# Attention: phi multiplied on POOL ahead of the inverses' spreading, its transposition and that of the inverses exchanged

## The chip, the cores and the metric

The kernel runs on one core of one Trainium2 chip. Its engines work side by side, each on its own queue of instructions in order: TensorE (PE: matrix products and transpositions into PSUM), VectorE (DVE), ScalarE (ACT), GpSimd (POOL) and SyncE (SP, which issues most DMAs). Semaphores tell one engine that another has finished. The metric is device microseconds (us) of one execution; the time before is the median of three runs.

## The reference, cut to what matters

Three stages follow each other: an attention with a memory term, a mixture of experts with one expert for each token, and a dense mixture with normalised weights. The change lies in the first, and this is all of it that it computes:

```python
B, H, S, D = 4, 8, 576, 64
scores = scale * np.matmul(q, k.transpose(0, 1, 3, 2))
scores = np.where(causal, -1000000000.0, scores)
a = np.exp(scores - scores.max(-1, keepdims=True))
a /= a.sum(-1, keepdims=True) + 1e-09
local = np.matmul(a, v)
q_p = np.where(q > 0, q, np.exp(q) - 1.0) + 1.0          # phi
mem_ret = np.einsum('bhsd,bhde->bhse', q_p, M_prev)
mem_norm = np.einsum('bhsd,bhd->bhs', q_p, z_prev)[..., None] + 1e-06
out = g * (mem_ret / mem_norm) + (1 - g) * local         # g = sigmoid(beta), one number a head
```

## The kernel before, in words

The attention works on 16 pairs of heads (u = 0 to 15; a batch has four). The 576 rows of a pair are four tiles of 128 and a tail of 64. A loop of 17 iterations is pipelined by one pair: iteration u computes the scores of pair u, the transpositions and the output product of pair u-1, and loads and prepares q, k and phi of pair u+1. An iteration has five steps, n = 0 to 4. Each step begins with a tile of scores (`score`, row tiles 3, 2, 1, 0 and the tail): PE multiplies (L233) and adds the mask (L235), DVE takes the row maximum (L237), ACT exponentiates and sums (L239).

The softmax isn't normalised before the output product. The unnormalised probabilities are transposed (`ptrans`, parts 0 to 7; L268, L276, L283, L289), phi is multiplied beforehand by the row's sum, the two products are added up in PSUM (`av`: L298 with the transposed phi `pT`, L306 with the transposed probabilities `pt`), and DVE multiplies the result by the transposed inverse sums `R` (L307). So two small tables are needed for the pair before: `pT` from phi, and `R` from the inverses `rr`, which POOL spreads over 64 columns a head. Both are made from `phi_c`, called at the end of iteration u-1, and each takes four transpositions on PE and an eviction from PSUM on ACT: `inverse` (L173, L174) at n = 1 and `trans(u - 1, 2)` (L191, L209) at n = 2.

For the next pair, `phi_a` makes phi: exp on ACT (L126), max(q, 0) on POOL (L127), then on DVE min(exp, 1) + max (L128), then the product with z on POOL (L131), which `phi_b` sums (L149, L150). The table of phi, `qp`, has two buffers in turn: L127 for pair u+1 writes the one that held pair u-1, so it can't begin before the transpositions of phi of pair u-1 (L191) have read it.

All transpositions and the output products of the attention share four PSUM buffers. The first part of the output product takes one of them, the parts of `ptrans` and the transposed q (evicted half by ACT, L206, half by DVE, L207) take others, so PE waits at a transposition until the buffer it is given has been evicted. By the semaphores of the built program, in an ordinary iteration L283 waits for the ACT eviction of part 2 (L270), L289 for L207, and the first L298 for the DVE eviction of part 3 (L270), and for `pT` as well where PE has not yet seen it.

The order inside the loop is not written out: a scheduler at build time puts each engine's instructions in a queue, by its own estimate of when operands are there. On the chip the queues are fixed. After each batch (in iterations 4, 8 and 12) POOL also issues four or five indirect DMAs that scatter tokens (L395); they stand in its queue ahead of L127 of the next iteration.

The lines that the change touches, in words of the kernel before: L162 makes the inverses of the sums (DVE), L164 spreads them (POOL, 128x512), L165 multiplies the memory's factor by the sums (DVE), and L167 multiplies phi by it (POOL, 128x512).

Of the kernel before, what the change touches and what calls it, by code (L numbers as in the profile page):

```python
# [14 lines left out]
ALU = mybir.AluOpType  # L15
# [3 lines left out]
B, H, S, D = 4, 8, 576, 64  # L19
# [8 lines left out]
def attention(ctx, tc, q, k, v, M_prev, z_prev, beta, xT, ident, router=None):  # L28
    nc = tc.nc
# [55 lines left out]
    zt, ld, ph, un = {}, {}, {}, {}  # L85
# [10 lines left out]
    def load_b(b):  # L96
        zt[b] = nat.tile([128, DM], F32, tag="z", name="zb", bufs=2)
        nc.sync.dma_start(zt[b], z_prev[b].rearrange("h d -> (h d)")[None, :].to_broadcast([128, DM]))
        for h in range(2):
            src = M_prev[b].rearrange("(a two) d e -> two d a e", two=2)[h]  # L100
            nc.sync.dma_start(Mb[b % 2][h * 64:(h + 1) * 64, :, h * 64:(h + 1) * 64], src)

    def load(u, names):

        b, a = divmod(u, NP)
        for nm in names:
            src = {"k": k, "q": q, "v": v}[nm]
            t = nat.tile([128, NT, 128], F32, tag=nm, name=f"{nm}n")
            for h in range(2):
                nc.sync.dma_start(t[:, :4, h * 64:(h + 1) * 64],  # L110
                                  src[b, 2 * a + h, :512, :].rearrange("(i p) d -> p i d", p=128))
            nc.sync.dma_start(t[:64, 4].rearrange("p (h d) -> p h d", h=2),
                              src[b, 2 * a:2 * a + 2, 512:, :].rearrange("h p d -> p h d"))
            ld[u, nm] = t
# [42 lines left out]
    def phi_c(u):  # L157

        su, n = un[u]["su"], nrm[u % 2]
        nc.vector.tensor_scalar(su[:, :4], su[:, :4], 1e-9, None, ALU.add)  # L160
        rc = sm.tile([128, 4, 2], F32, tag="rc", name="rc", bufs=2)
        nc.vector.reciprocal(rc, su[:, :4])  # L162
        rr = un[u]["rr"] = tmp.tile([128, 4, 128], F32, tag="rr", name="rr")
        nc.gpsimd.tensor_copy(rr.rearrange("p i (h d) -> p i h d", h=2), rc[:, :, :, None].to_broadcast([128, 4, 2, D]))  # L164
        nc.vector.tensor_tensor(n[:, :4], n[:, :4], su[:, :4], ALU.mult)  # L165
        pv = ph[u][1][:, :4].rearrange("p i (h d) -> p i h d", h=2)
        nc.gpsimd.tensor_tensor(pv, pv, n[:, :4, :, None].to_broadcast([128, 4, 2, D]), ALU.mult)  # L167

    def inverse(u):

        p = ps_t.tile([128, 512], F32, tag="t", name="rp_")
        for i in range(4):
            nc.tensor.transpose(p[:, i * 128:(i + 1) * 128], un[u]["rr"][:, i], ident)  # L173
        nc.scalar.copy(Rs[u % 2][:, :512], p)  # L174

    def phi_t(u):
        if "pT" not in un[u]:
            un[u]["pT"] = tr.tile([128, S], F32, tag="pT", name="pT")
        return un[u]["pT"]

    def trans(u, part):


        qt = qTp[u % 2]
        p = ps_t.tile([128, 512], F32, tag="t", name="tp")
        if part == 0:
            un[u] = {"kT": tr.tile([128, S], F32, tag="kT", name="kT"), "P": {}}
        if part < 3:
            src = (ld.get((u, "k")), ld.get((u, "q")), ph[u][1] if u in ph else None)[part]
            for i in range(4):  # L190
                nc.tensor.transpose(p[:, i * 128:(i + 1) * 128], src[:, i], ident)  # L191
        else:
            src = []
            if part == 3:
                src += [ld[u, "k"], ld[u, "q"]]
                if u > 0:
                    src.append(ph[u - 1][1])
            else:
                src += [ph[u][1]]
            for n, t in enumerate(src):  # L200
                nc.tensor.transpose(p[:, n * 64:(n + 1) * 64], t[:64, 4], ident[:64, :64])

        if part == 0:
            nc.vector.tensor_copy(un[u]["kT"][:, :512], p)
        elif part == 1:
            nc.scalar.activation(qt[:, 256:512], p[:, 256:], AF.Copy, scale=0.125)  # L206
            nc.vector.tensor_scalar(qt[:, :256], p[:, :256], 0.125, None, ALU.mult)  # L207
        elif part == 2:
            nc.scalar.copy(phi_t(u)[:, :512], p)  # L209
        elif part == 3:  # L210
            nc.vector.tensor_copy(un[u]["kT"][:, 512:], p[:, 0:64])
            nc.scalar.activation(qt[0:64, 512:576], p[0:64, 64:128], AF.Copy, scale=0.125)
            nc.vector.tensor_scalar(qt[64:128, 576:640], p[64:128, 64:128], 0.125, None, ALU.mult)
            if u > 0:
                nc.vector.tensor_copy(phi_t(u - 1)[:, 512:], p[:, 128:192])
        else:
            nc.vector.tensor_copy(phi_t(u)[:, 512:], p[:, 0:64])

    def score(u, i):

        b, a = divmod(u, NP)
        kT = un[u]["kT"]
        qt = qTp[u % 2]
        s = ps_s.tile([128, 2, 512], F32, tag="s", name="s")
        nm = sm.tile([128, 2], F32, tag="nm", name="nm")
        if i == 3:
            un[u]["su"] = sm.tile([128, NT, 2], F32, tag="su", name="su", bufs=2)
        sums = un[u]["su"][:, i]
        if i < 4:
            w = (i + 1) * 128  # L230
            for h in range(2):
                r = slice(h * 64, (h + 1) * 64)
                nc.tensor.matmul(s[:, h, :w], qt[r, i * 128:(i + 1) * 128], kT[r, :w], start=True, stop=False)  # L233
            for h in range(2):
                nc.tensor.matmul(s[:, h, w - 128:w], idb, mk, start=False, stop=True)  # L235
            P = pp.tile([128, 2, w], F32, tag=f"P{i}", name=f"P{i}")
            nc.vector.tensor_reduce(nm, s[:, :, :w], AX.X, ALU.max, negate=True)  # L237
            for h in range(2):
                nc.scalar.activation(P[:, h], s[:, h, :w], AF.Exp, bias=nm[:, h:h + 1], accum_out=sums[:, h:h + 1])  # L239
        else:  # L240
            w = 288
            for h in range(2):
                nc.tensor.matmul(s[:, h, :w], qt[:, 512:640], kT[:, h * w:(h + 1) * w], start=True, stop=(h == 0))
            nc.tensor.matmul(s[:, 1, 224:288], idb, mk2, start=False, stop=True)
            P = pp.tile([128, 2, w], F32, tag=f"P{i}", name=f"P{i}")
            nc.vector.tensor_reduce(nm[:, 0:1], s[:, :, :w], AX.XY, ALU.max, negate=True)
            nc.scalar.activation(P, s[:, :, :w], AF.Exp, bias=nm[:, 0:1], accum_out=sums[:, 0:1])
        un[u]["P"][i] = P
# [72 lines left out]
    for u in range(NU + 1):  # L321
        sc, ex = u < NU, u > 0
        if u + 1 < NU:
            load(u + 1, "v")
        if u + 2 < NU:
            if (u + 2) % NP == 0:
                load_b((u + 2) // NP)
            load(u + 2, "kq")
        if u == 2 and rt:
            rt.clear()  # L330
        for n in range(5):
            if sc:
                score(u, (3, 2, 1, 0, 4)[n])
                if n == 4:
                    phi_c(u)
            if ex:
                if n == 0:
                    norm(u - 1)
                    ptrans(u - 1, 5)
                    ptrans(u - 1, 4)  # L340
                elif n < 3:
                    ptrans(u - 1, 2 * n - 2)
                    ptrans(u - 1, 2 * n - 1)
                    if n == 1:
                        inverse(u - 1)
                    else:
                        trans(u - 1, 2)
                elif n == 3:
                    ptrans(u - 1, 6)
                    ptrans(u - 1, 7)  # L350
                    av(u - 1, 0)
                else:
                    av(u - 1, 1)
                    if rt and u % NP == 0:
                        rt.batch(u // NP - 1, ps_t)
            if sc:
                if n == 0:
                    phi_b(u)
                elif n == 2:
                    gate_v(u)  # L360
                elif n == 3 and u + 1 == NU:
                    trans(u, 4)
            if u + 1 < NU:
                if n < 2:
                    trans(u + 1, n)
                elif n == 3:
                    trans(u + 1, 3)
                    phi_a(u + 1)
        if ex:
            del un[u - 1]  # L370
# [918 lines left out]
```

## Time and profile before

| what | us |
|---|---|
| median of three runs | 2078.39 (2077.78 to 2081.22) |
| the profiled execution | 2079.47 |
| its span | 2077.8 |
| PE busy, whole span | 2041.4 (98%) |
| DVE busy | 1482.1 (71%) |
| ACT busy | 854.6 (41%) |
| POOL busy | 777.2 (37%) |

The last output product of the attention ends its last eviction at about 277 us of the span; all that follows is the two mixtures. The span is 1.67 us shorter than the execution's time, which counts what lies around it. A row of the timeline has the start in us from the span's start, the time taken, engine, line, operation, output<-input, shapes, count, and in square brackets the idle time of that engine just before, with what ended it. PEld is the loading of weights, the part of PE that a wait is seen on first.

### The profile page before, as it was taken

The numbers are of one execution on the slowest core, as the hardware profiler recorded it, in microseconds if no ns is written. First come the engines' busy times: TensorE is split into PE (matmuls) and PEld (weight loads), VectorE is DVE, ScalarE is ACT, GpSimd is POOL, SyncE is SP. The second block draws the span as 40 slices with busy tenths as digits, with TensorE's granted clock in tenths as the row PEclk, the third lists the DMA queues.
The fourth block names the chain that finished last, engine by engine and source line by source line (L and its number), as shares of the span: only waits on it lengthen the run. The fifth ranks groups of instructions, "written<-read, shape, count | busy, mean of one in ns | idle before, by whom it ended". The sixth has DMA issues, their size and how long they took to land.

```text
span 2077.8 us, 31530 instructions
## 1 busy us (share of the span) xinstructions
PE 2041.4 (98%) x11526; PEld 1770.6 (85%) x11528; DVE 1482.1 (71%) x2573; ACT 854.6 (41%) x1808; POOL 777.2 (37%) x800
## 2 busy tenths in 40 slices
PE   8999999999899999999999999999999999999998
PEld 5666569999798899889889899889988889889987
DVE  7787757666786776667786677677678676677775
ACT  5556546555634333333343333333334433333332
POOL 6666511000133344344464334334345333333432
PEclk8999999999999999999999999999999999999999
DMA  7332147665612233444432222222223222222221
GB/s 189 87 71 78 33 152 231 203 212 170 209 52 61 62 69 73 61 66 77 61 106 68 61 74 69 62 73 70 62 61 112 62 63 80 61 63 80 62 62 40
DMA packets 238520, 187.35 MB, mean 90 GB/s; under 512 B 71440, under 2 KB 194320, under 8 KB 238352
## 3 DMA queue, kind: packets, MB, share of 16 engines
q1 hardware_dynamic: 229008, 171.48, 30.2%
q0 software_dynamic: 3520, 9.46, 1.3%
q10 hardware_dynamic: 5824, 4.25, 0.7%
q8 instruction: 95, 1.56, 0.3%
q14 instruction: 73, 0.60, 0.1%
HBM read 171.51 MB, written 13.64 MB: 89 GB/s over the span
## 4 chain that ended last, share of the span: by engine, by line
PE 46%; issue 16%; POOL 8%; DVE 3%; ACT 1%; POOLq 0%; DVEq 0%; ACTq 0%
PE y L1093 24%; PE prod L1022 21%; POOL T L914 4%; POOL w1l L908 3%; DVE u L1036 0%; DVE w2l L908 0%; DVE c L1036 0%; POOL out_dram L395 0%; DVE hl L1045 0%; PE lq L1134 0%; DVE S2l L908 0%; DVE A11l L908 0%; DVE A12l L908 0%; DVE csum L1167 0%; ACT hh L1040 0%
## 5 line engine op out<-in xcount | busy, mean ns | idle before, releaser
L1040 ACT ACTIVATE hh<-c 128x384 fp32r<-128x384 f32 x384 | 202.1, 526 | 837.5 <-DVE c L1036 837.4
L908 POOL TENSOR_TENSOR w1l<-T,w1h 128x1024 fp32r<-128x1024 f32 x94 | 226.9, 2414 | 850.2 <-ACT w1h L908 850.2
L1093 PE MATMUL y<-w2h,hh 128*128 128x512 f32 x1152 | 453.4, 394 | 0.0
L1093 PE MATMUL y<-w2l,hh 128*128 128x512 f32 x1152 | 453.3, 394 | 0.0
L1093 PE MATMUL y<-w2h,hl 128*128 128x512 f32 x1152 | 452.5, 393 | 0.0
L1045 DVE SCALAR_TENSOR_TENSOR hl<-c,hh 128x384 fp32r<-128x384 f32 x384 | 415.7, 1100 | 1.4 <-ACT hh L1040 1.0
L1036 DVE TENSOR_TENSOR c<-prod,u 128x384 f32<-128x384 f32 x288 | 160.2, 556 | 157.2 <-PE prod L1022 156.6
L1093 PEld LDWEIGHTS y<-w2h,hh 128*128 128x128 f32 x1152 | 216.2, 188 | 32.8
L1093 PEld LDWEIGHTS y<-w2h,hl 128*128 128x128 f32 x1152 | 216.2, 188 | 28.6
L1093 PEld LDWEIGHTS y<-w2l,hh 128*128 128x128 f32 x1152 | 216.3, 188 | 28.0
L914 POOL TENSOR_TENSOR T<-r,T 128x256 f32<-128x256 f32 x188 | 157.9, 840 | 14.0 <-issue 6.9
L914 POOL TENSOR_TENSOR T<-r 128x256 f32<-128x256 f32 x188 | 159.1, 847 | 7.2
L1036 DVE TENSOR_TENSOR u<-prod,u 128x384 f32<-128x384 f32 x192 | 106.0, 552 | 58.1 <-PE prod L1022 57.6
L1036 DVE TENSOR_TENSOR u<-prod,p 128x384 f32<-128x384 f32 x96 | 53.5, 557 | 126.9 <-PE prod L1022 126.7
L908 DVE TENSOR_TENSOR w2l<-r,w2h 128x512 fp32r<-128x512 f32 x188 | 137.0, 729 | 0.5 <-ACT w2h L908 0.5
L908 ACT CAST w2h<-r 128x512 fp32r<-128x512 f32 x188 | 106.7, 610 | 0.0
L908 DVE TENSOR_TENSOR w1l<-r,w1h 128x512 fp32r<-128x512 f32 (+1 forms) x188 | 104.7, 557 | 0.0
L1036 DVE TENSOR_TENSOR c<-prod,p 128x384 f32<-128x384 f32 x96 | 53.4, 556 | 68.9 <-PE prod L1022 64.2
L908 ACT CAST w1h<-T 128x1024 fp32r<-128x1024 f32 x94 | 97.0, 1032 | 1.0 <-POOL T L914 1.0
L1050 ACT COPY p<-prod 128x384 f32<-128x384 f32 x96 | 46.1, 480 | 121.3 <-PE prod L1022 121.3
L1104 DVE SCALAR_TENSOR_TENSOR acc<-y,P,acc 128x512 f32<-128x512 f32 x126 | 92.4, 744 | 4.3 <-PE y L1093 4.3
L908 ACT CAST w1h<-r 128x512 fp32r<-128x512 f32 (+1 forms) x188 | 94.5, 502 | 0.0
(386 smaller groups left out, 4210.4 us busy)
## 6 DMA issues: line engine op xcount, KB each, us to landing
r<-in_moe_w_dram SPq DMA_DIRECT2D x188, 512.0 KB, 4.6
r<-in_moe_w_dram SPq DMA_DIRECT2D x188, 256.0 KB, 3.0
xr<-xs_sorted SPq DMA_DIRECT2D x22, 256.0 KB, 5.1
kn<-in_k_dram SPq DMA_DIRECT2D x32, 128.0 KB, 2.7
qn<-in_q_dram SPq DMA_DIRECT2D x32, 128.0 KB, 2.8
vn<-in_v_dram SPq DMA_DIRECT2D x32, 128.0 KB, 2.6
xs_sorted<-zrow ACTq DMA_DIRECT2D x16, 256.0 KB, 3.4
zb<-in_z_prev_dram SPq DMA_DIRECT2D x4, 256.0 KB, 3.6
```

Of the source, the lines that this page charges most:

```text
L908: return (lambda: nc.scalar.copy(hi, src)), (lambda: eng.tensor_tensor(lo, src, hi.bitcast(F32), ALU.subtract))
L914: sub = lambda i, a, b: (lambda: nc.gpsimd.tensor_tensor(T[:, i], a, b, ALU.subtract))
L1022: nc.tensor.matmul(p, a[:, kd], b[:, kd], start=(i == 0), stop=(i == 5))
L1036: nc.vector.tensor_tensor(st[o], a, st[b], ALU.add)
L1040: nc.scalar.activation(hh[:, f, a * HT:(a + 1) * HT], st[o], AF.Relu)
L1045: nc.vector.scalar_tensor_tensor(hl[:, f, w], st[o], 0.0, hh[:, f, w].bitcast(F32), ALU.max, ALU.subtract)
L1050: nc.scalar.copy(st["p1"], p)
L1093: nc.tensor.matmul(yt[t], a[:, f, t * 128:(t + 1) * 128], b[:, f], start=(j == 0 and f == 0 and i == 0), stop=(j == NJ - 1 and f == 1 and ...
L1104: nc.vector.scalar_tensor_tensor(acc[t], yt[t], P[:, m, e:e + 1], acc[t], ALU.mult, ALU.add)
```

## The change

In `phi_c` the product of phi and its factor is put ahead of the spreading of the inverses, on DVE and on POOL. In the loop the two calls are exchanged: `trans(u - 1, 2)` is made at n = 1 and `inverse(u - 1)` at n = 2. No instruction is added or taken away.

```diff
         nc.vector.tensor_scalar(su[:, :4], su[:, :4], 1e-9, None, ALU.add)
+        nc.vector.tensor_tensor(n[:, :4], n[:, :4], su[:, :4], ALU.mult)
+        pv = ph[u][1][:, :4].rearrange("p i (h d) -> p i h d", h=2)
+        nc.gpsimd.tensor_tensor(pv, pv, n[:, :4, :, None].to_broadcast([128, 4, 2, D]), ALU.mult)
         rc = sm.tile([128, 4, 2], F32, tag="rc", name="rc", bufs=2)
         nc.vector.reciprocal(rc, su[:, :4])
         rr = un[u]["rr"] = tmp.tile([128, 4, 128], F32, tag="rr", name="rr")
         nc.gpsimd.tensor_copy(rr.rearrange("p i (h d) -> p i h d", h=2), rc[:, :, :, None].to_broadcast([128, 4, 2, D]))
-        nc.vector.tensor_tensor(n[:, :4], n[:, :4], su[:, :4], ALU.mult)
-        pv = ph[u][1][:, :4].rearrange("p i (h d) -> p i h d", h=2)
-        nc.gpsimd.tensor_tensor(pv, pv, n[:, :4, :, None].to_broadcast([128, 4, 2, D]), ALU.mult)
...
                     if n == 1:
+                        trans(u - 1, 2)
+                    else:
                         inverse(u - 1)
-                    else:
-                        trans(u - 1, 2)
```

On PE, in iteration 7, the four transpositions of the inverses (`rr`, L173) and the four of phi (`qp`, L191) change places; this is the place at n = 1:

```order
 L268 MATMUL tp2_1666<-ident_58,P2_1468 128x128
 L268 MATMUL tp2_1666<-ident_58,P3_1430 128x128
-L173 MATMUL rp__1672<-ident_58,rr_1582 128x128 x4
+L191 MATMUL tp_1672<-ident_58,qp_1370 128x128 x4
 L191 MATMUL tp_1678<-ident_58,qn_1419 128x128 x4
 L233 MATMUL s_1685<-kT_1456,qTp1_136 128x256 x2
```

Nothing else moves there; the transpositions of the inverses stand at n = 2, where those of phi stood, and all other rows of PE in this iteration keep their places.

On DVE the scheduler gives a new order. In iteration 7, `qp_1750` is phi of pair 8, the next one, `tp_1678` the transposed q, `tp2_1700` part 3 of the transposed probabilities, `nm_1686` the maximum of the scores of n = 2:

```order
 L237 TENSOR_REDUCE nm_1651<-s_1650 128x2
 L270 COPY pt_1625<-tp2_1666 128x512
+L128 SCALAR_TENSOR_TENSOR qp_1750<-ex_1749,qp_1750 128x512
+L128 SCALAR_TENSOR_TENSOR qp_1750<-ex_1749,qp_1750 64x128
 L237 TENSOR_REDUCE nm_1686<-s_1685 128x2
 L207 TENSOR_SCALAR qTp0_134<-tp_1678 128x256
 L270 COPY pt_1625<-tp2_1700 128x384
-L128 SCALAR_TENSOR_TENSOR qp_1750<-ex_1749,qp_1750 128x512
+L149 TENSOR_REDUCE nrm0_142<-ex_1749 128x8
 L237 TENSOR_REDUCE nm_1714<-s_1713 128x2
 L285 COPY pt_1625<-tp2_1723 128x4x64
 L290 COPY pt4_1626<-tp2_1730 64x128
```

Both rows of L128 have moved from behind the evictions L207 and L270 to ahead of them. The same order stands in iterations 3, 4, 6, 7, 8, 10, 11, 12 and 14. In iteration 2 the two rows keep their places. In iteration 1 the long one goes ahead of L237 and L207 as here, and L149 too goes ahead of L207.

In iterations 5, 9 and 13, behind a batch's scatter, DVE's queue changes thus (iteration 5; `qp_1370` is phi of pair 6, `tp_1298` the transposed q):

```order
 L237 TENSOR_REDUCE nm_1271<-s_1270 128x2
 L270 COPY pt_1245<-tp2_1286 128x512
+L128 SCALAR_TENSOR_TENSOR qp_1370<-ex_1369,qp_1370 128x512
+L207 TENSOR_SCALAR qTp0_134<-tp_1298 128x256
 L237 TENSOR_REDUCE nm_1306<-s_1305 128x2
-L207 TENSOR_SCALAR qTp0_134<-tp_1298 128x256
 L270 COPY pt_1245<-tp2_1320 128x384
-L128 SCALAR_TENSOR_TENSOR qp_1370<-ex_1369,qp_1370 128x512
+L128 SCALAR_TENSOR_TENSOR qp_1370<-ex_1369,qp_1370 64x128
 L237 TENSOR_REDUCE nm_1334<-s_1333 128x2
```

Here the long row of L128 alone has moved ahead of L207; POOL's queue, in which L127 stands behind the scatter, is as it was. In iterations 1, 5, 9 and 13 it is L283 that waits for L207 in the changed program, and no longer L289.

## Rows read from the trace of the kernel before

**Rows 1.** Busy time by stretch: PE, PEld, DVE, ACT, POOL, PEclk, DMA share, GB/s.
```profile
120.00:160.00 40.00, 39.11 (x287) 24.35 (x284) 31.16 (x88) 22.95 (x67) 22.86 (x27) 1.00 0.29 68
```
**Rows 2.** The view of waits: who waited for whom, us in total, times, longest.
```profile
DVE qp L128 <- POOL qp L127: 19.6, 14, 2.5
...
PEld x L298 <- ACT pT L209: 8.1, 15, 1.8
```
**Rows 3.** Timeline of iteration 7, all engines, from n = 1 to n = 3.
```profile
124.68 0.47 PEld L173 LDWEIGHTS rp__1672<-ident,rr 128*128 128x128 f32 x4
124.74 0.39 POOL L142 TENSOR_TENSOR vn<-vn,om 64x128 f32<-64x128 f32 x1
...
126.72 0.69 DVE L237 TENSOR_REDUCE nm<-s 128x2 f32<-128x512 f32 x1 [1.03 <-PE s L235]
...
127.07 0.47 PEld L191 LDWEIGHTS tp<-ident,qp 128*128 128x128 f32 x4
...
127.33 0.41 DVE L207 TENSOR_SCALAR qTp<-tp 128x256 f32<-128x256 f32 x1
...
127.66 0.55 DVE L270 COPY pt<-tp 128x384 f32<-128x384 f32 x1
...
127.93 1.98 POOL L127 TENSOR_SCALAR qp<-qn 128x512 f32<-128x512 f32 x2 [2.79 <-issue]
...
128.20 0.42 PEld L283 LDWEIGHTS tp<-ident,P 128*128 128x128 f32 x4
...
128.59 0.11 PEld L289 LDWEIGHTS tp<-ident,P 128*64 128x64 f32 x1
...
128.99 0.30 PEld L298 LDWEIGHTS x<-pT,Mb 128*128 128x128 f32 x2 [0.29 <-ACT pT L209]
...
129.46 0.77 DVE L128 SCALAR_TENSOR_TENSOR qp<-ex,qp 128x512 f32<-128x512 f32 x1 [1.25 <-POOL qp L127]
...
130.30 1.27 POOL L131 TENSOR_TENSOR ex<-qp,zb 128x512 f32<-128x512 f32 x1 [0.40 <-DVE qp L128]
...
131.01 0.71 DVE L128 SCALAR_TENSOR_TENSOR qp<-ex,qp 64x128 f32<-64x128 f32 x1
```
**Rows 4.** Groups by line and shape, 40 to 260 us: busy us, mean ns.
```profile
L127 POOL TENSOR_SCALAR qp<-qn 128x512 f32<-128x512 f32 x13 | 19.4, 1495 | 27.7 <-issue 16.4 <-PE tp L191 10.2 <-PE tp L289 1.1
```
**Rows 5.** Timeline of DVE in iteration 0, where POOL does not run L131 beside L128.
```profile
11.67 0.27 DVE L128 SCALAR_TENSOR_TENSOR qp<-ex,qp 64x128 f32<-64x128 f32 x1
11.87 0.67 DVE L149 TENSOR_REDUCE nrm<-ex 128x8 f32<-128x512 f32 x1
```
**Rows 6.** Timeline of iteration 1.
```profile
29.41 0.47 PEld L173 LDWEIGHTS rp__440<-ident,rr 128*128 128x128 f32 x4
...
30.75 1.04 POOL L141 TENSOR_TENSOR vn<-vn,om 128x512 f32<-128x512 f32 x1
...
33.83 0.42 PEld L283 LDWEIGHTS tp<-ident,P 128*128 128x128 f32 x4
```
**Rows 7.** Timeline of iteration 5, behind the first scatter.
```profile
98.38 0.60 PE L283 MATMUL tp<-ident,P 128*128 128x128 f32 x4
...
99.25 2.01 POOL L127 TENSOR_SCALAR qp<-qn 128x512 f32<-128x512 f32 x2
...
102.50 0.81 PE L298 MATMUL x<-pT,Mb 128*128 128x320 f32 x2 [0.35 <-DVE pt L290]
```
**Rows 8.** Timeline of iteration 9, behind the second scatter.
```profile
164.78 0.96 POOL L395 DMA_INDIRECT xs_sorted<-xr,row  x1 [0.30 <-ACT pt L270]
...
167.47 0.69 PE L298 MATMUL x<-pT,Mb 128*128 128x256 f32 x2 [1.57 <-ACT pT L209]
```
**Rows 9.** Timeline of iteration 15, the first without phi of a next pair.
```profile
261.98 0.30 PEld L298 LDWEIGHTS x<-pT,Mb 128*128 128x128 f32 x2 [0.81 <-ACT pT L209]
```
**Rows 10.** Timeline of PE behind the routed experts' main loop.
```profile
518.33 1.00 PE L824 MATMUL h1r<-w1l,xh 128*128 128x256 f32 x4 [1.98 <-PEq L889]
```
**Rows 11.** Busy time by stretch, directly after that wait.
```profile
518.50:522.00 3.50, 3.50 (x18) 3.50 (x18) 2.42 (x5) 2.38 (x6) 0.00 (x0) 0.51 0.81 261
```

## Prediction

> **What bounds the kernel now.** I read the busy time by stretch first. In 40 us of the attention's steady part PE is busy 39.11 at the full granted clock, while DVE, ACT and POOL have 9 to 17 us of slack each [rows 1]. So only an instruction that PE would wait for, or a loss of its clock, changes the time; the work of the other engines is free until PE stands behind it. The mixtures have no edited line and are taken as they are.
>
> The view of waits then names two things that touch the change [rows 2]. PEld's first L298 waits for ACT's eviction of the transposed phi, `pT`: 8.1 us in 15 times. That is the wait which the exchange can take away. And DVE's L128 waits for POOL's L127, 19.6 us in 14 times. Before, this second wait costs PE nothing. The timeline of iteration 7 shows why: DVE stands idle for 1.25 us ahead of L128 at 129.46, but L207 and the last L270, which free PSUM buffers for PE, were issued at 127.33 and 127.66, ahead of it in the queue [rows 3]. PE's own wait in that iteration is 0.29 us, for `pT`.
>
> **The change part by part.** No instruction is added; what counts is order. Three edits go together at nothing: the product on POOL made ahead of the spreading, the tiny DVE product, and the exchange of four transpositions for four of the same size. The first two are work of engines with slack, the third leaves PE's sum unchanged. Their bounds are 0 and, were phi late at n = 1, a wait like that for `pT`, 1.8 us at the longest [rows 2]; I take 0.
>
> What the exchange sets off is an earlier L127. It is bound to the transpositions of phi, since it overwrites the buffer that they read: they start at 127.07, L127 at 127.93, 0.86 us later [rows 3]. Put at the place of L173, which starts at 124.68, they would release it at 125.54; POOL is free by then, as L142 ends at 124.74 + 0.39 = 125.13. The long L127 takes 1.49 us [rows 4], so phi's maximum is there at 127.03. That is 2.4 us earlier, but the new order puts both rows of L128 ahead of L237, L207 and L270 of DVE, where before they came behind them. L237 began at 126.72. Now it must wait for L128, and behind it wait L207 and L270, and behind these PE's L289 and L298.
>
> Ordinary iterations (3, 4, 6, 7, 8, 10, 11, 12 and 14: nine), by the durations of [rows 3]:
> - L128 long starts 127.07 (0.04 after L127, as before: 129.46 against 127.93 + 1.49), takes 0.77; a next row on DVE begins 0.08 before its predecessor ends (127.33 against 126.72 + 0.69), so L128 short begins at 127.76. It takes 0.27 when POOL doesn't work beside it [rows 5]: 128.03.
> - L237 0.69 less 0.08: 128.64. L207 0.41: to 128.97. L270 0.55 less 0.08: to 129.44; by the 0.08 not always gained, to 129.52. Before, L270 ended at 128.21.
> - PE's L289 stood at 128.59 and goes to some 129.05, and L298, which needs that L270, goes from 128.99 (its 0.29 for `pT` included) to about 129.57: +0.58. Nine times: **+5.2 us**.
> Bounds: if PE does not wait at all it gains the 0.29, -2.6 us over nine; from above, L128 short takes 0.71 beside POOL's L131 as it did at 131.01 [rows 3], +0.44 each, +9.2 us in all. I stay at 0.27, because it would now be issued just ahead of L131 and not behind it.
>
> Iteration 1: PE's first transpositions of the slot start at 29.41, but POOL is busy with L141 up to 30.75 + 1.04 = 31.79 [rows 6]. L127 ends at 33.28, its short row (1.98 - 1.49 = 0.49) at 33.77, L142 and L155 at 0.39 each at 34.55, L131 (1.27) at 35.82, L149 (0.67 [rows 5]), now ahead of L207, at 36.53, L207 at 36.86. L283, which now waits for L207, goes from 33.83 [rows 6] to 36.91: **+3.1**.
>
> Iteration 5: L127 stands behind the scatter and keeps its 99.25 [rows 7]. It ends at 100.74, L128 at 101.55, L207 at 101.88, and L283 starts at 101.93 where PE had it at 98.38: 3.6 late. Later in the iteration a wait of 0.35 for L290 [rows 7] and one of 0.3 for `pT` are absorbed: **+3.0**.
>
> Iterations 9 and 13: L395 ends at 164.78 + 0.96 = 165.74 [rows 8]; L127 to 167.27, L128 to 168.08, L207 to 168.41, L283 at 168.46 and L298 0.50 behind it (128.20 to 128.99 less 0.29 [rows 3]) at 168.96. Before, L298 started at 167.47 after waiting 1.57 for `pT`, a wait that goes [rows 8]: +1.5. Iteration 13 has the same order and I give it the same: **+3.0** for both. Bounds for these four iterations together: 0, if PE finds other buffers free, to 13, if each costs the whole 3.1 to 3.6.
>
> Gains where no L128 stands in the way: 0.81 in iteration 15 [rows 9], about 0.29 each in 2 and 16: **-1.4**. Sum so far: 5.2 + 3.1 + 3.0 + 3.0 - 1.4 = **+12.9 us**.
>
> The clock: in the steady part it is granted in full [rows 1], so it can't gain. Four waits of some 3 us are new on PE. The nearest row is the wait of 1.98 us in the experts' stage [rows 10], behind which the clock was granted at 0.51 (1.2 GHz in place of 2.4) for 3.5 us [rows 11], that is 1.7 us lost. So 0 to 4 x 1.7 = 6.8 us; I take two falls, for the two longest waits (iterations 1 and 5): **+3.4**. The total is +16.3. The sum is made on the profiled execution, 2079.47 us (span 2077.8), 0.05% above the median of 2078.39; added to the median it gives **2095 us**.
>
> A rule that speaks against this change: the short L128 is a DVE instruction with two inputs in SBUF, and POOL's L131 reads SBUF; the row of L128 that ran beside L131 took 0.71 us [rows 3] where the one without took 0.27 [rows 5]. The Trainium skill, SBUF — State Buffer, "Who interferes with whom", says that such a pair contends for a shared read port, that this is an exclusive lock, and that the order of issue decides who blocks. The trace agrees that DVE is slowed; that it can be shut out for all of L131's 1.27 us no row here shows. If DVE is first, the sum stays; if POOL is first, it is the first rival below.
>
> **The rivals.**
> 1. POOL gets ahead at L128 short. L131 would start some 0.07 us after L128 long ends, at 127.91, and last to 129.18; L128 short would end 1.2 us later than in my sum, and with it L207 and L270. Nine times 1.2 is +10.8: 2106 us. For it: the 0.71 at 131.01 [rows 3]. Against: DVE's next row starts without a gap, POOL's needs a semaphore. Chance 0.16.
> 2. Faster: the exchange does what is wanted. `pT` is a slot earlier, the 8.1 us of PEld's wait [rows 2] go, and L128 finds its input there, so that no eviction is late: 2070 us. It decides if L127 ends before 125.95 or so, when L128's 0.77 could be over by L237's 126.72. With 125.54 + 1.49 it misses that by 1.1 us, unless POOL is released sooner than 0.86 us after the slot's start or PE runs later against POOL than in this trace. Chance 0.08.
> 3. No change: L207 and L270 are late but PE has other work up to them in ordinary iterations, so the 0.29 each is gained (-2.6, and -1.4 in iterations 2, 15 and 16), and only the iterations 1, 5, 9 and 13 lose, about half of my 9.1, with no fall of the clock: +0.6, 2079 us. For it: four PSUM buffers in turn. Against: each is wanted again within a step. Chance 0.12.
>
> **How the numbers follow.** My forecast has 0.64: 2095, by itself 2087 (no fall of the clock, ordinary iterations at less than 0.2) to 2102 (four falls, some L128 at 0.71). What the measurement of this kernel can tell is about 0.2%, 4.2 us. Faster has rival 2, 0.08. Same has rival 3 and the weakest end of the forecast: 0.13. Slower has the rest, 0.79. The range goes from 2080 to 2107: it takes in rival 1 at its upper end and leaves out rival 2, most of rival 3, and a little above.
>
> **What would show it.** Right: in iteration 7 DVE's idle time ahead of L128 stands before L237, not after L270; PE waits at L289 or L298 for DVE's L207 or L270, about 0.6 us; L298's wait for `pT` is gone from the view of waits; in iterations 1 and 5 L283 waits about 3 us for L207, perhaps with half the clock behind it. The two mixtures keep their length. Wrong: L127 starting much sooner or later than 0.86 us after the slot; no PE wait on L207 or L270; L128 short at 1.2 us or more (rival 1); the waits as I say but a span within 4 us of before, which would mean that PE makes up later what it loses here.

## The result, and the profile after

The changed kernel takes 2096.75 us (median of four runs, 2094.83 to 2097.15), the kernel before beside it 2078.27 (four runs); the ratio is 1.0083, 95% interval 1.0071 to 1.0095. The forecast was 2095, slower. The profiled execution has a span of 2095.4 us, 17.6 more than before.

I take the start of DVE's first L270 in each iteration as its mark and set the marks of the two traces side by side. By the mark of iteration 16, 17.2 of the 17.6 us have arisen, 0.45 of them ahead of the mark of iteration 1; the mixtures, behind the last L307, take 1801.7 us, and took 1800.9 before. The ordinary place first: the timeline of iteration 7 after the change, all engines.

```profile
134.93 0.47 PEld L191 LDWEIGHTS tp<-ident,qp 128*128 128x128 f32 x4
...
135.77 0.40 POOL L142 TENSOR_TENSOR vn<-vn,om 64x128 f32<-64x128 f32 x1
...
136.13 1.98 POOL L127 TENSOR_SCALAR qp<-qn 128x512 f32<-128x512 f32 x2
...
137.65 0.97 DVE L128 SCALAR_TENSOR_TENSOR qp<-ex,qp 128x512 f32<-128x512 f32 x2 [1.72 <-POOL qp L127]
...
138.55 0.67 DVE L237 TENSOR_REDUCE nm<-s 128x2 f32<-128x512 f32 x1
139.15 0.40 DVE L207 TENSOR_SCALAR qTp<-tp 128x256 f32<-128x256 f32 x1
139.48 0.54 DVE L270 COPY pt<-tp 128x384 f32<-128x384 f32 x1
139.60 0.11 PEld L289 LDWEIGHTS tp<-ident,P 128*64 128x64 f32 x1 [0.74 <-DVE qTp L207]
...
140.07 0.30 PEld L298 LDWEIGHTS x<-pT,Mb 128*128 128x128 f32 x2 [0.35 <-DVE pt L270]
```

The idle time of DVE ahead of L128 has moved from behind L270 [rows 3] to ahead of L237, and grown from 1.25 to 1.72 us. Behind it everything is late in a row: L237, L207, L270, and so PE's L289 and L298. By the slot I mean the place at n = 1 where the exchanged transpositions stand. L298 starts 5.14 us after the slot's first row here, 4.31 before (128.99 against 124.68 in [rows 3]). L127 starts 1.20 us after the slot and not 0.86, because POOL's L142 ends only at 136.17. In this, iteration 7 is one of two exceptions: in seven of the nine ordinary iterations L127 starts 0.86 or 0.87 us after the slot's first row, in iteration 11 it starts 1.34 us after it.

The view of waits of the changed kernel (who waited for whom, us in total, times, longest):

```profile
DVE qp L128 <- POOL qp L127: 29.9, 14, 5.2
...
PE tp L283 <- DVE qTp L207: 13.4, 4, 3.7
...
PEld tp L289 <- DVE qTp L207: 4.4, 9, 0.9
...
PEld x L298 <- DVE pt L270: 3.2, 9, 0.4
```

The wait of L298 for `pT` [rows 2] has no row any more. In its place stand nine waits for L207 and L270, in the nine ordinary iterations, and four long ones of L283, in iterations 1, 5, 9 and 13. Iteration 5, behind the scatter:

```profile
103.28 0.96 POOL L395 DMA_INDIRECT xs_sorted<-xr,row  x1 [0.30 <-issue]
104.27 2.01 POOL L127 TENSOR_SCALAR qp<-qn 128x512 f32<-128x512 f32 x2
105.83 0.77 DVE L128 SCALAR_TENSOR_TENSOR qp<-ex,qp 128x512 f32<-128x512 f32 x1 [5.16 <-POOL qp L127]
106.53 0.41 DVE L207 TENSOR_SCALAR qTp<-tp 128x256 f32<-128x256 f32 x1
...
107.09 1.08 PE L283 MATMUL tp<-ident,P 128*128 128x128 f32 x4 [3.68 <-DVE qTp L207]
```

L283's four transpositions take 1.08 us here and 0.60 before [rows 7]: the clock has fallen. Busy time by stretch, of the stretches behind the four waits (PE, PEld, DVE, ACT, POOL, PEclk, DMA share, GB/s):

```profile
37.00:41.00 4.00, 3.48 (x16) 2.23 (x16) 2.06 (x8) 1.37 (x7) 0.45 (x1) 0.57 0.22 76
105.50:112.50 7.00, 5.41 (x21) 3.64 (x22) 5.23 (x16) 3.00 (x12) 3.10 (x5) 0.51 0.06 14
180.50:184.50 4.00, 4.00 (x17) 2.49 (x16) 2.76 (x12) 2.26 (x10) 1.50 (x2) 0.57 0.30 66
249.00:252.50 3.50, 3.33 (x15) 2.19 (x15) 2.73 (x8) 2.07 (x9) 1.49 (x2) 0.51 0.00 0
```

The clock fell to half at each of the four waits, in the wait or up to 1.5 us behind its end; before, the attention had full clock from 27.5 us on.

### The profile page after: what moved, and what is told of

The parts are those of the page before. It is cut to its first block, busy times and chain, and to the rows that moved or that the text cites. A ratio compares the mean times of both kernels' runs of the same rounds, so it can differ in the third digit from the quotient of the medians.

```text
span 2095.4 us, 31517 instructions
## 1 busy us (share of the span) xinstructions
PE 2047.7 (98%) x11526; PEld 1776.4 (85%) x11528; DVE 1468.4 (70%) x2573; ACT 855.3 (41%) x1808; POOL 779.7 (37%) x800
## 4 chain that ended last, share of the span: by engine, by line
PE 45%; issue 16%; POOL 8%; DVE 3%; ACT 0%; POOLq 0%; ACTq 0%; DVEq 0%
PE y L1093 24%; PE prod L1022 21%; POOL T L914 4%; POOL w1l L908 3%; DVE u L1036 0%; DVE w2l L908 0%; DVE c L1036 0%; POOL out_dram L395 0%; DVE hl L1045 0%; DVE S2l L908 0%; DVE A11l L908 0%; DVE A12l L908 0%; PE lq L1134 0%; DVE csum L1167 0%; PE lg L1146 0%
```

## The experiments

Eleven kernels ran, each beside the kernel before. Theory A is the prediction's: DVE stands still at L128 for POOL, the evictions stand behind it, PE waits for them, and its clock falls behind the long waits. Where a diff says `behind` or `after_all`, it adds an ordering edge without a semaphore: the scheduler must put the one DVE instruction later in the queue than the other, and nothing waits for anything new.

**Holding L128 behind the eviction, in all iterations, in four, in the rest.**

```diff
-            nc.vector.scalar_tensor_tensor(p, e, 1.0, p, ALU.min, ALU.add)
+            behind(u, nc.vector.scalar_tensor_tensor(p, e, 1.0, p, ALU.min, ALU.add))
...
+    def behind(u, i):
+        if u > 1: after_all(tc, i, late, mybir.DependencyClass.NoSync)
```

Here u is the pair whose phi is made, one ahead of the iteration, and `late` holds DVE's eviction of part 3 of the same iteration (the line that fills it is left out). The second run has `u % 4 == 2 and u > 1` as its condition, the third `u % 4 != 2 and u > 1`.

All: 

> The changed kernel, with one thing added: an ordering edge without a semaphore puts both rows of L128 behind the DVE eviction of part 3 (L270) of the same iteration, from iteration 1 on. PE's order is the same as in the changed kernel; POOL, ACT and DVE keep their instructions. Theory A (the loss comes from L128 standing ahead of the evictions L207 and L270 on DVE while its input from POOL is late, with the clock's falls behind the long waits): the whole loss goes, and the wait for pT stays away; 2072 to 2079 us, no L283 or L289 waiting for L207, full clock from 28 to 300 us. Rival B (the exchange itself costs: the inverses a slot later, so that L307 and the x buffer are late, or POOL's new order): most of the loss stays, 2090 us or more, with waits on L307 or on R.

Four: 

> The changed kernel with L128 held behind L270 only in iterations 1, 5, 9 and 13; the others keep the changed order. Theory A: the four long waits (3.0 to 3.7 us each in the trace of the changed kernel) and the four stretches at half clock go, the ordinary waits of about 0.5 us stay: 2097 less 12 to 14, 2083 to 2085 us. If the clock's falls cost nothing (rival C: PE behind the wait is bound by other engines anyway): only the waits' 10 us less what the kernel before waited there, 2088 to 2090. Rival B: 2094 or more.

The rest: 

> The complement: L128 held behind L270 in all iterations but 1, 5, 9 and 13. Theory A: the ordinary 0.5 us in nine iterations and the wait for pT go, the four long waits and their clock stay: 2097 less 5 to 8, 2089 to 2092 us. Together with the other half the two savings should add up to that of holding all, within 3 us. Rival B: 2094 or more.

| held in | us, median | ratio to before, 95% |
|---|---|---|
| all iterations | 2068.45 | 0.9951 (0.9938 to 0.9965) |
| 1, 5, 9, 13 | 2077.86 | 0.9990 (0.9981 to 0.9999) |
| the others | 2086.12 | 1.0037 (1.0023 to 1.0050) |

The kernel before had 2079.54 beside them. PE's order is the changed kernel's in all three. Holding all gives back more than the change had cost, and ends below the range expected. The exchange is kept and the loss is gone, so rival B falls. Against before the changed kernel stood at +18.5 us, the three at -11.1, -1.7 and +6.6: the four iterations are worth 20.2 us, the others 11.9, together 32.1 against 29.6, additive within the 3 us. Both parts are larger than I expected (12 to 14, and 5 to 8). By the marks, the four iterations of the second run give 18.8 us: they end 4.0 us below the kernel before, where I had brought them back no further than to it. The nine others of the third run give 8.0; the rest lies outside them, in part in iterations 5 and 13, where the profiled execution had a shorter fall of the clock and none (2.7 us together). Rival C, a clock that costs nothing, would have left the second run at 2088 to 2090. Iteration 7 with L128 held, PE and DVE:

```profile
123.32 0.41 DVE L207 TENSOR_SCALAR qTp<-tp 128x256 f32<-128x256 f32 x1
123.65 0.55 DVE L270 COPY pt<-tp 128x384 f32<-128x384 f32 x1
124.11 0.68 DVE L128 SCALAR_TENSOR_TENSOR qp<-ex,qp 128x512 f32<-128x512 f32 x1
124.58 0.11 PEld L289 LDWEIGHTS tp<-ident,P 128*64 128x64 f32 x1
...
124.69 0.30 PEld L298 LDWEIGHTS x<-pT,Mb 128*128 128x128 f32 x2
```

Neither L128 nor PE has idle time in brackets: the wait for `pT` of [rows 3] is gone and nothing has taken its place.

**Is it the place in the queue, or the late input?** L127 goes to DVE; L127 and L128 stay ahead of the evictions.

```diff
-            (nc.gpsimd if u else nc.vector).tensor_scalar(p, qn, 0.0, None, ALU.max)
+            nc.vector.tensor_scalar(p, qn, 0.0, None, ALU.max)
```

> The changed kernel with L127 moved from POOL to DVE, which has only L128's input in its own hands then; PE's order stays that of the changed kernel, and L127 and L128 still stand ahead of L237, L207 and L270 in DVE's queue in the ordinary iterations. Theory A (what costs is that DVE stands still for POOL, not that L128 takes its turn early): the idle time ahead of L128 goes, also behind the scatters, the four long waits and the clock's falls go, and what is left is DVE's own work ahead of the evictions; 2068 to 2079 us. Rival E (the mere work of phi ahead of the evictions makes them late): L127 adds to it, so 2095 or more.

Measured: 2069.61 us, ratio 0.9954 (0.9940 to 0.9967). DVE in iteration 7:

```profile
122.06 0.54 DVE L127 TENSOR_SCALAR qp<-qn 128x512 f32<-128x512 f32 x2
122.52 0.88 DVE L128 SCALAR_TENSOR_TENSOR qp<-ex,qp 128x512 f32<-128x512 f32 x2
...
123.32 0.68 DVE L237 TENSOR_REDUCE nm<-s 128x2 f32<-128x512 f32 x1
```

DVE works from 122.06 to L237 at 123.32 without a gap, on 1.3 us more than stood there before the change, and the loss is gone. So rival E falls: the early place costs nothing by itself that this run can tell, only with an input that is late. One wait and one fall of the clock were left, in iteration 9:

```profile
162.53 0.30 PEld L298 LDWEIGHTS x<-pT,Mb 128*128 128x128 f32 x2 [1.99 <-DVE pt L270]
```

```profile
164.00:168.00 4.00, 4.00 (x14) 2.29 (x14) 2.47 (x12) 1.83 (x7) 1.87 (x3) 0.57 0.35 78
```

The expectation had all falls gone. DVE stood idle for 2.20 us ahead of that L270, in the kernel before for 2.10 us at the same place, in holding all for 0.27; what it waited for is not shown.

**The two halves of the change.** Only the exchange with L128 unheld and held, and only the product first:

```diff
                     if n == 1:
-                        inverse(u - 1)
-                    else:
                         trans(u - 1, 2)
+                    else:
+                        inverse(u - 1)
```

This is the exchange alone, on the kernel before; with the hold of the first experiment it is the second run. The product alone is the other part of the change's diff, with the calls as before.

> Only the two calls are exchanged; the product of phi and its factor stays behind the spreading on POOL, as in the kernel before. PE's and ACT's orders are those of the changed kernel, and L128 stands ahead of the evictions as there. Theory A: the same loss, 2093 to 2098 us, and a wait of L191 for phi's product at n = 1 at most in the order of 1 us an iteration, since the product comes 0.6 us later. Rival D (the loss hangs on POOL's order of product and spreading): back to 2080 or less.

> Only the two calls are exchanged, with L128 held behind L270 as in the first experiment; the product of phi stays behind the spreading on POOL. Theory A: phi's product comes 0.6 us later than with the product first, and the transpositions of phi at n = 1 still find it done; within 3 us of holding all, 2067 to 2072. Rival D (the product's place on POOL carries the gain): 2076 or more, with L191 waiting for POOL at n = 1.

> Only the product of phi is put ahead of the spreading, the calls at n = 1 and n = 2 stay as before; PE's and ACT's orders are those of the kernel before. Theory A: no engine that PE waits for gains or loses, the inverses are 1 us later for transpositions that come a whole step later; 2076 to 2081, no difference that can be measured. Rival F (the inverses are now late at n = 1): 2085 or more, with L173 waiting for the spreading.

Measured: exchange alone 2099.11 (1.0089, 1.0076 to 1.0103), exchange with L128 held 2068.27 (0.9944, 0.9931 to 0.9958), product alone 2080.27 (1.0000, 0.9990 to 1.0009). The first is 1 us over the range expected. The product's place does nothing in any of them; loss and gain both hang on the exchange.

**A third buffer, and both cures at once.**

```diff
-        qp = tmp.tile([128, NT, 128], F32, tag="qp", name="qp")
+        qp = tmp.tile([128, NT, 128], F32, tag="qp", name="qp", bufs=3)
```

This stands on holding all; the second run has L127 on DVE on holding all, with two buffers.

> Holding all as in the first experiment, and a third buffer for phi, so that L127 does not wait for the transpositions of phi of the pair before. Theory A: L127 is earlier, but once L128 is behind the evictions nothing on PE waits for it; the same as holding all within 3 us, 2066 to 2071. If L127's release still cost PE time somewhere: faster by more than 4 us, 2064 or less.

> Both cures at once: L127 on DVE and L128 held behind L270. Theory A: each takes the same stall away, so they do not add up; 2066 to 2071 us, the same as either within 3 us. If the late start of L127 behind the scatters still cost something: 2064 or less.

Measured: 2068.84 (0.9944, 0.9931 to 0.9958) and 2068.53 (0.9955, 0.9942 to 0.9969). With the third buffer L127 runs an iteration earlier, and DVE's idle time ahead of L128 in iterations 5 and 9 of holding all (2.45 and 2.08 us) is gone, yet the time is the same. Once the evictions no longer stand behind L128, it does not matter when its input comes. Counting L127 on DVE and the exchange alone with L128 held, five kernels now stand at 2068 to 2070 us, about 0.5% below the kernel before and 1.3% below the changed one; none went lower.

**The clock by itself.** First a base in which the long waits of iterations 5, 9 and 13 stay (the first added line, on holding the others; `m` is the short L128, `last` the eviction L290; L149 is tied likewise, in a line left out here), then the same with idle products in them (the second added line).

```diff
+        after_all(tc, m, last if u % 4 == 2 else [], mybir.DependencyClass.NoSync); ph[u] = ex, qp
...
-                nc.tensor.matmul(s[:, h, w - 128:w], idb, mk, start=False, stop=True)
+                nc.tensor.matmul(s[:, h, w - 128:w], idb, mk, start=False, stop=True); [nc.tensor.matmul(s[:, h, 128:], zeros[:, :128], zeros[:, :384], start=True, stop=True) for _ in range(9 if i == 0 and u % 4 == 1 < u else 0)]
```

> The kernel of the third experiment (L128 held in the ordinary iterations only), with the short row of L128 and L149 also put behind L290 in iterations 1, 5, 9 and 13. There only the long row of L128 still stands ahead of L207. It is the base of the next run. Theory A: iteration 1 loses the delay by L131 and L149 (its L207 no longer waits for them), the waits of 3 us or more in 5, 9 and 13 stay, with a fall of the clock behind two or three of them; 2081 to 2085 us.

> The same, with 18 idle products of zeros (384 columns each, about 2.9 us by those of 128 columns at full clock) in PE's queue after the mask of n = 3 in iterations 5, 9 and 13, directly ahead of the L283 that waits; they write a part of the scores' buffer that nobody reads. The orders of POOL and ACT are those of the run before, DVE's differs only behind L290. If the clock's fall is a cost of its own (about 1.5 us each, as the changed order's iterations with and without a fall differ): L283 starts at the same time or up to 0.3 us later, no half clock behind it, 3 to 5 us faster than the run before. If it costs nothing, or falls all the same: within 1 us of the run before, or slower.

Measured: base 2088.15 (1.0056, 1.0041 to 1.0071), filled 2078.79 (1.0007, 0.9998 to 1.0016). The base missed its range by 3 us: all four iterations fell to half clock, three of them for some 7 us. Iteration 1, which was to lose its delay, is still 4.9 us longer than in holding all by the marks: its wait is shorter, but the fall behind it is one of the three. The fill saved 9.4 us and not 3 to 5. L283 of iteration 5 of the base, and the stretches behind its three waits:

```profile
103.79 1.09 PE L283 MATMUL tp<-ident,P 128*128 128x128 f32 x4 [3.49 <-DVE qTp L207]
```

```profile
103.50:107.00 3.50, 3.21 (x15) 2.12 (x15) 2.85 (x8) 1.98 (x9) 1.61 (x2) 0.53 0.02 5
171.50:178.50 7.00, 6.19 (x23) 3.95 (x24) 4.79 (x16) 3.02 (x12) 2.77 (x4) 0.51 0.14 34
239.50:247.00 7.50, 6.19 (x24) 4.05 (x25) 5.22 (x16) 2.19 (x10) 3.27 (x5) 0.54 0.00 0
```

The same of the filled kernel:

```profile
104.58 0.63 PE L283 MATMUL tp<-ident,P 128*128 128x128 f32 x4 [0.54 <-DVE qTp L207]
```

```profile
98.00:112.00 14.00, 13.46 (x94) 8.01 (x92) 7.87 (x25) 6.67 (x22) 9.53 (x11) 1.00 0.39 118
166.00:184.00 18.00, 17.45 (x128) 11.03 (x125) 11.21 (x29) 9.58 (x31) 11.98 (x14) 1.00 0.35 100
236.00:254.00 18.00, 17.75 (x132) 11.62 (x130) 15.39 (x39) 10.35 (x35) 10.78 (x13) 1.00 0.08 17
```

PE still waits for L207, 0.54 us behind the fill, but the clock stays full and the transpositions take 0.63 in place of 1.09 us. From iteration to iteration (starts of the first L270) the filled trace gains 1.5 us behind the fall of 3.5 us, 2.9 and 2.8 behind those of some 7. Iteration 1, which got no idle products, has its fall in both traces. Added useless work made the program faster: a fall of the clock is a cost of its own. The two spans differ by 6.6 us, the medians by 9.4: the profiled execution of the filled kernel was the slowest of its eleven, 2081.49 us, 2.7 above their median, and that of the base was its median.

## Why the prediction was right, and where two of its terms were not

By the same marks, the 17.6 us of the changed trace beside the forecast's terms:

| part | forecast, us | measured, us |
|---|---|---|
| ordinary iterations 3, 6, 7, 10, 11, 14 | 6 x 0.58 = 3.5 | 3.8 (0.47 to 0.98 each) |
| iterations 4, 8, 12 | 3 x 0.58 = 1.7 | -0.6 |
| iterations 1, 5, 9, 13, waits and clock | 9.1 + 3.4 = 12.5 | 4.3 + 4.9 + 2.9 + 2.8 = 14.8 |
| iterations 2, 15, 16 | -1.4 | -1.7 |
| ahead of iteration 1, and behind the last L307 | 0 | 1.3 |
| sum | 16.3 | 17.6 |

**The steps that held.** L127 is released by the transpositions of phi, DVE waits for it with the evictions behind, and PE waits at L289 and L298 in the nine iterations named and at L283 in the four. In the six ordinary iterations of the table the size held as well: 0.47 to 0.53 us in four, 0.83 and 0.98 in iterations 7 and 11, where POOL was late for L127. With the clock taken off (below: 1.5 us each, 2.7 in iteration 5) the four long waits cost 2.8, 2.2, 1.4 and 1.3 us, where the forecast had 3.1, 3.0, 1.5 and 1.5. Rival 1 is refuted by the row of L128 above: both rows together took 0.97 us, which is 0.77 and 0.27 with the usual overlap, and the short one took 0.27 or 0.28 us in all nine ordinary iterations. DVE was first and POOL's L131 did not hold it. Of before, the short row ends 0.15 us after L131 (131.72 against 131.57 in [rows 3]), and so it does, by 0.14 or 0.15 us, in all 13 iterations from 2 to 14; where POOL is first the row looks shut out until L131 ends. The trace so agrees with the Trainium skill (SBUF — State Buffer, "Who interferes with whom"), by which such a pair contends for an exclusive lock and the order of issue decides who blocks.

**The clock's term was mis-sized.** "I take two falls, for the two longest waits" gave 3.4 us. There were four. Three lasted some 3.4 us, at the 1.5 us each that the fill showed; the one in iteration 5 lasted from 105.6 to 112.5, with 5.4 us of it behind the wait's end at 107.09, so 2.7. That makes 7.2, an estimate from these rows, over the upper bound of 6.8. My nearest row [rows 11] showed only the short form.

**The ordinary term was too large where a batch ends.** In iterations 4, 8 and 12 PE waited before the change already, at the router's first product for DVE's L307. Before and after, end of iteration 4:

```profile
85.90 0.14 PEld L488 LDWEIGHTS lq<-xT,wg 128*32 128x32 f32 x2 [1.45 <-DVE xT L307]
```

```profile
90.28 0.14 PEld L488 LDWEIGHTS lq<-xT,wg 128*32 128x32 f32 x2 [0.51 <-DVE xT L307]
```

With L128 and L149 done early DVE reaches L307 sooner: before, it worked up to L307 without a gap, now it stands idle for 0.78 us ahead of it and waits for PE's last product. So 0.94 us of PE's waiting comes back there, 1.24 and 0.94 in iterations 8 and 12. I had looked for what becomes late and not for what DVE's earlier work makes early. The errors, +3.8 for the clock, -2.3 here, -1.5 at the long waits (not followed further) and +1.3 outside the loop, nearly cancel: the mechanism was right, but that the time came within 2 us is in part luck.

**Rival 2 had the right price for a kernel that I did not forecast.** It gave 2070 us, should the exchange take the wait for `pT` away with no eviction late. That is what every cured kernel measures.

## What to carry to other kernels

When an exchange releases one engine earlier, look at what a scheduler then moves forward on the next engine: an instruction whose input comes from a slow engine holds everything queued behind it, and buffers that TensorE needs may be among it. An early place in an in-order queue is worth something only if the input is there as early; an ordering edge, or the input made on the same engine, turned this loss of 0.8% into a gain of 0.5%. Price a wait of TensorE with the clock behind it, at the longest fall that the traces show, and look too for waits which the moved work ends.

## What was not expected of the hardware

The half clock at a wait lasted about 3.4 us in some executions and about 6.8 in others, at the same place of the same order on PE. In iteration 9 of the changed kernel it lasted 3.4 us (180.50:184.50 above, after a wait of L283 of 3.48 us); with the exchange alone, where L283 waited 3.35 us, 6.8:

```profile
176.50:184.00 7.50, 5.49 (x22) 3.67 (x23) 5.27 (x16) 3.58 (x13) 3.53 (x5) 0.54 0.12 35
```

Nor does each long wait bring it: in the run with L128 held in the others, iteration 13 waited 3.18 us and kept the full clock,

```profile
239.83 0.63 PE L283 MATMUL tp<-ident,P 128*128 128x128 f32 x4 [3.18 <-DVE qTp L207]
```

```profile
234.00:248.00 14.00, 10.82 (x80) 6.74 (x80) 7.67 (x25) 5.52 (x19) 9.88 (x11) 1.00 0.22 77
```

while in the base for the fill, iteration 1 waited 1.35 us at L283 and 0.39 at L298 and then ran at half clock for 6.8:

```profile
34.12 0.42 PEld L283 LDWEIGHTS tp<-ident,P 128*128 128x128 f32 x4 [1.35 <-POOL qp L155]
...
35.02 0.42 PEld L298 LDWEIGHTS x<-pT,Mb 128*128 128x128 f32 x2 [0.39 <-ACT pt L270]
```

```profile
35.00:42.00 7.00, 6.98 (x22) 3.76 (x24) 4.18 (x16) 2.58 (x10) 2.10 (x4) 0.51 0.55 170
```

What decides between these was not settled. And L127 for 128x512, 1.50 us on POOL in the changed kernel, took 0.45 us on DVE (means of 12 and 13).
